# Strassen's algorithm for most of the first batch's up projections, and partial sums kept in a PSUM bank

## The chip, the cores and the metric

The kernel runs on one core of a Trainium2 chip. The metric is the device time of one execution in microseconds, from a few runs of the same kernel. The core has a matrix engine (PE in the profile, its weight loads shown as PEld), a vector engine (DVE), a scalar engine (ACT), a general engine (POOL), and SP, which here issues the transfers. Each works through a queue of its own; they wait for one another through semaphores. PE writes to PSUM[...]; DVE and ACT read it from there.

## What is computed

A clustered attention, then a bilinear feed-forward network on its output. The reference, cut to what matters:

```python
# q, k, v: (4, 8, 768, 64); centroids: (8, 16, 64)
q_assign = argmax(einsum('bhsd,hcd->bhsc', q_n, c_n))
k_assign = argmax(einsum('bhsd,hcd->bhsc', k_n, c_n))
mask = q_assign[:, :, :, None] == k_assign[:, :, None, :]
scores = where(mask, scale * q @ k.T, -1e9)
x = softmax(scores) @ v            # to (3072, 512)
# w_a, w_b: (512, 1536); w_out: (1536, 512)
out = ((x @ w_a) * (x @ w_b)) @ w_out
```

The weights come as 64-bit floats and are rounded to 32-bit floats in the kernel.

## The kernel before

**Attention.** There are 4 batches and 4 pairs of heads in each, 16 pairs `p`. The 768 queries of a pair are two halves `hf` of 384, the keys six tiles `j` of 128. One unit is one half against one key tile for both heads of the pair; a group `g` is two units, so a pair has 6 groups and there are 96. For each group the main loop has PE compute the scores (`score`, L548: one-hot cluster vectors, then q and k), ACT the exponentials (L557), PE the product with v for the group before (`weigh`, L589), and DVE, from the fifth pair on with POOL, the sums over keys (`add_up`, L578). When a half is complete, PE sums over partitions (`denominators`, L612), ACT copies (L617), DVE transposes, inverts and transposes back (`normalize`, L632 to L639), and POOL multiplies the output with it (L644). At the start of the next group ACT reads the inverse once more (`check_inverses`, L652). The preparation of the next pair (transposes, similarities L365, cluster choice, one-hot vectors L479 to L485) is spread over the six groups of a pair.

**Weights.** The 36 weight tiles of 128 x 512 are loaded one after another into two `raw` tiles and rounded by `round_w`: four DVE steps (L280, L283, L287, L290), of which the first two read the high halves of the raw words and the last the low halves; ACT takes the absolute value of the high halves into a tile of its own (`size`, L294); POOL adds the rest (L295); and in the next group `flush_w` has DVE multiply the weight with whether its size is at least `SMALLEST` (L302), which sets subnormal weights to 0. A table `due` says in which group each tile is rounded.

**Feed-forward.** It is cut into pieces, kept in the queue `ffn`, and each group takes pieces until a budget of columns (`PER_GROUP`) is used up. Pieces of one batch run beside the attention of the next. For batches 1 to 3 the up projections use Strassen's algorithm in Winograd's form (`ffn_ups`): the features are taken in pairs of 128-column tiles, and each of 6 indices and 2 weights makes 7 products of four blocks instead of 8. DVE forms the combinations of x (`combine_x`, L739 and L751) and of the weights (L766). PE writes each product to one of three PSUM banks of the pool `ps_m` in turn. ACT copies the first product out (L807), and DVE adds every other one where it belongs (L793). For the second weight, POOL multiplies the two factors of the network (L798). Batch 0's up projections are plain (`ffn_block`): every piece is one feature tile for one half of the rows, with four chunks of the inner dimension in one bank; ACT copies the first factor (L690) and DVE multiplies (L694). The first half's first pieces start when its own rows are ready, three groups before the second half's. All down projections (`ffn_downs`) use Strassen's algorithm.

**Order and buffers.** The order of each engine's instructions is that of the program. Scores have two tiles of two banks (`ps_s`), the outputs one bank (`ps_o`), and the remaining three banks (`ps_m`) serve similarities, denominators and all feed-forward products in turn. All feed-forward matmuls go through `in_halves` (L663), which splits the 128 output rows into two halves; the profile has two records for each matmul call in full precision.

Of the kernel before, what the change touches and what calls it, by code (L numbers as in the profile page):

```python
# [28 lines left out]
SMALLEST = 1.125 * 2.0 ** -15  # L29

# [5 lines left out]
def kernel(  # L36
# [97 lines left out]
    with tc.If(redo > 0):  # L134
        with ExitStack() as slow:
            long_path(nc, tc, slow, c, q, k, v, out)


def short_path(nc, tc, ctx, c, cn, centroids_in, casts, n_far, q, k, v,
# [32 lines left out]
    sizep = pool("sizep", 2)  # L172
# [96 lines left out]
    flush = []  # L269

    def round_w(i):
        flush_w()
# [20 lines left out]
        size = sizep.tile([P, WN], FP32, name="size")  # L293
        nc.scalar.activation(out=size, in_=halves(FP32)[:, :, 1], func=AF.Abs)  # L294
        nc.gpsimd.tensor_tensor(out=w, in0=w, in1=rest, op=ALU.add)  # L295
        flush.append((w, size))

    def flush_w():

        while flush:  # L300
            w, size = flush.pop(0)
            nc.vector.scalar_tensor_tensor(out=w, in0=size, scalar=SMALLEST,  # L302
                                           in1=w, op0=ALU.is_ge, op1=ALU.mult)

    stat = zero.tile([P, 4 * NPAIR], FP32, name="stat")
# [23 lines left out]
    def keep_busy(n):  # L329

        for _ in range(n):
            nc.tensor.transpose(out=idle[:, 0:P], in_=ident, identity=ident)  # L332

# [25 lines left out]
    def prep_sim(p):  # L359
# [3 lines left out]
        ps = ps_m.tile([P, 512], FP32, name="m")  # L363
# [238 lines left out]
    def denominators(p, hf):  # L602


        ps = ps_m.tile([P, 512], FP32, name="m")
# [52 lines left out]
    def in_halves(ps, lhsT, rhs, start, stop):  # L658


        for a in range(2):
            half = slice(a * D, (a + 1) * D)
            nc.tensor.matmul(out=ps[half], lhsT=lhsT[:, half], rhs=rhs,  # L663
                             start=start, stop=stop)
# [7 lines left out]
    def ffn_block(b, blk):  # L672

        box = {}
        t0 = blk * HB

        def up(w_sb, f):
            ps = ps_m.tile([P, 512], FP32, name="m")
            for ch in range(NCH):
                in_halves(ps[:, 0:HB], w_sb[:, ch, f * P:(f + 1) * P],  # L680
                          xTs[b][:, ch, t0:t0 + HB],
                          start=(ch == 0), stop=(ch == NCH - 1))
            return ps

        def piece_a(f):
            if f == 0:
                box["h"] = hp_.tile([P, NF, HB], FP32, name="h")
            ps = up(wa_sb, f)
# [3 lines left out]
        def piece_b(f):  # L692
            ps = up(wb_sb, f)
            nc.vector.tensor_tensor(out=box["h"][:, f, :], in0=box["a"],  # L694
                                    in1=ps[:, 0:HB], op=ALU.mult)

        ups = [(NCH * HB, lambda f=f, piece=piece: piece(f))
               for f in range(NF) for piece in (piece_a, piece_b)]
        return ups, box
# [10 lines left out]
    def room():  # L710
        if not W:
            W["raw"] = [rawp.tile([P, 2 * WN], FP32, name="raw") for _ in range(2)]
            W["size"] = [sizep.tile([P, WN], FP32, name="size") for _ in range(2)]
            W["comb"] = combp.tile([P, 2 * P], FP32, name="comb")
        return W["raw"], W["size"], W["comb"]
# [4 lines left out]
    def up_room():  # L720
        raw, size, comb = room()
        quarter = lambda t: t[:, 0:2 * HB].rearrange("p (c t) -> p c t", c=2)
        beside = lambda t: t[:, 2 * HB:].rearrange("p (c f) -> p c f", c=2)
        chunks = lambda t: [t[:, c, :] for c in range(2)]
        W["T3"], W["T2"] = chunks(quarter(raw[0])), chunks(quarter(raw[1]))
        W["T4"] = [t[:, 0:HB] for t in size]
        W["slots"] = [chunks(beside(raw[0])), chunks(beside(raw[1])),
                      chunks(comb.rearrange("p (c f) -> p c f", c=2)),
                      [t[:, HB:] for t in size]]

    def combine_x(b):
        up_room()
        x = xTs[b]
        for c in range(2):
            x11, x12 = x[:, c, 0:HB], x[:, c, HB:S]
            x22 = x[:, c + 2, HB:S]
            t2, t3 = W["T2"][c], W["T3"][c]
            for out, l, r in ((t3, x22, x12), (x12, x12, x11), (t2, x22, x12)):
                nc.vector.tensor_tensor(out=out, in0=l, in1=r, op=ALU.subtract)  # L739

    def ffn_ups(b, h):

        x = xTs[b]
        X = {"11": [x[:, c, 0:HB] for c in (0, 1)],
             "T1": [x[:, c, HB:S] for c in (0, 1)],
             "21": [x[:, c, 0:HB] for c in (2, 3)],
             "22": [x[:, c, HB:S] for c in (2, 3)]}

        def combine_t4():
            for c in range(2):  # L750
                nc.vector.tensor_tensor(out=W["T4"][c], in0=W["T2"][c],  # L751
                                        in1=X["21"][c], op=ALU.subtract)

        def products(w_sb, i, is_a):
            N2 = NF // 2
# [5 lines left out]
            def combine(name, l, r, op):  # L761

                at = {"S1": 1, "S2": 2, "S3": 0, "S4": 3}[name]
# [9 lines left out]
            def half_2():  # L773
# [3 lines left out]
                W["slots"] = [s[1], s[2], s[0], s[3]]  # L777

            def product(l, r):
                ps = ps_m.tile([P, 512], FP32, name="m")  # L780
                rhs = X[r] if r in X else W[r]
                for c in range(2):
                    in_halves(ps[:, 0:HB], A[l][c], rhs[c],
                              start=(c == 0), stop=(c == 1))
                return ps[:, 0:HB]
# [6 lines left out]
            def add(out, in0, ps, op=ALU.add):  # L792
                nc.vector.tensor_tensor(out=out, in0=in0, in1=ps, op=op)  # L793
# [7 lines left out]
            def p1():  # L801
# [3 lines left out]
                ps = product("11", "11")  # L805
                box["11"] = place(0, i)
                nc.scalar.copy(out=box["11"], in_=ps)  # L807

            def p6():
                ps = product("S2", "T2")  # L810
                box["12"] = place(1, i)
                add(box["12"], box["11"], ps)

            def p2_ahead():
                box["P2"] = product("12", "21")

            def p2():
# [552 lines left out]
```

## Time and profile before

| | |
|---|---|
| median of 3 runs (lowest, highest) | 1049.01 us (1048.68, 1049.04) |
| the profiled execution | 1048.94 us, of which its span is 1047.2 us |
| granted TensorE clock | 0.999 of full speed |

In a table of windows a line has the window, its length, and for each engine the busy time and, in brackets, the number of instructions; then the clock, the share of time in which the transfer engines work, and what they moved.

```profile
78.00:104.00 26.00, 26.00 (x171) 11.15 (x168) 22.82 (x42) 15.34 (x28) 4.86 (x4) 1.00 0.46 95
...
208.00:234.00 26.00, 26.00 (x164) 11.48 (x162) 21.69 (x34) 10.28 (x19) 13.76 (x13) 1.00 0.24 77
...
468.00:494.00 26.00, 26.00 (x168) 11.17 (x168) 17.14 (x33) 6.26 (x12) 11.30 (x12) 1.00 0.31 47
```

The order of engines is PE, PEld, DVE, ACT, POOL. The first window lies in the attention of batch 0 without any feed-forward work, the second in the first batch's up projections, while weights are still being rounded, the third in the second batch's Strassen products. PE's ends are modelled, so 26 of 26 us says that matmuls follow one another closely, not that they are at their peak.

In the page's groups of instructions, a line has the source line, the engine, the operation, what it writes and reads, its shape and count; then busy time and mean duration in ns; then the idle time of the engine just before, and who ended it. In a timeline, it is the start, the time, the engine, the line, the operation, and in square brackets the idle time before and who ended it.

### The profile page before, as it was taken

The numbers are of one execution on the slowest core, as the hardware profiler recorded it, in microseconds if no ns is written. First come the engines' busy times: TensorE is split into PE (matmuls) and PEld (weight loads), VectorE is DVE, ScalarE is ACT, GpSimd is POOL, SyncE is SP. The second block draws the span as 40 slices with busy tenths as digits, with TensorE's granted clock in tenths as the row PEclk, the third lists the DMA queues.
The fourth block names the chain that finished last, engine by engine and source line by source line (L and its number), as shares of the span: only waits on it lengthen the run. The fifth ranks groups of instructions, "written<-read, shape, count | busy, mean of one in ns | idle before, by whom it ended". The sixth has DMA issues, their size and how long they took to land.

```text
span 1047.2 us, 17953 instructions
## 1 busy us (share of the span) xinstructions
PE 1034.4 (99%) x7163; PEld 510.5 (49%) x7163; DVE 710.3 (68%) x1404; ACT 259.8 (25%) x500; POOL 355.8 (34%) x329
## 2 busy tenths in 40 slices
PE   9999999999999999999999999999999999999997
PEld 5444444444445554444444555444444565444575
DVE  6778877887857457676766736767655846776752
ACT  4665333233321221221212121222121200000000
POOL 1111345555543332453545422453344310212200
PEclk9999999999999999999999999999999999999999
DMA  7334243525130221203020030200000000000001
GB/s 182 87 84 88 85 107 105 126 71 140 63 49 21 43 38 29 32 5 46 5 46 6 25 62 25 46 1 20 1 4 2 15 28 22 1 1 1 2 32 34
DMA packets 120523, 46.49 MB, mean 44 GB/s; under 512 B 106608, under 2 KB 115824, under 8 KB 120432
## 3 DMA queue, kind: packets, MB, share of 16 engines
q1 hardware_dynamic: 120016, 44.85, 18.4%
q8 instruction: 58, 0.95, 0.4%
q10 hardware_dynamic: 416, 0.43, 0.1%
q14 instruction: 33, 0.27, 0.1%
HBM read 37.78 MB, written 6.29 MB: 42 GB/s over the span
## 4 chain that ended last, share of the span: by engine, by line
PE 93%; DVE 4%; issue 1%; POOL 1%; ACT 0%; DVEq 0%; POOLq 0%
PE m L663 61%; PE s L548 15%; PE O L589 12%; PE m L612 2%; PE m L365 1%; DVE raw L739 1%; POOL xT L644 1%; DVE raw L766 0%; PE m L346 0%; DVE xT L739 0%; PE O L332 0%; DVE ha L793 0%; DVE acc L639 0%; DVE raw L883 0%; DVE acc L578 0%
## 5 line engine op out<-in xcount | busy, mean ns | idle before, releaser
L557 ACT ACTIVATE pt<-s 128x768 f32<-128x768 f32 x192 | 145.2, 808 | 307.0 <-PE s L548 245.3
L578 POOL TENSOR_TENSOR acc<-acc,pt 128x384 f32<-128x384 f32 x144 | 152.8, 1075 | 57.8 <-ACT pt L557 41.8
L798 POOL TENSOR_TENSOR h<-h,ha 128x384 f32<-128x384 f32 x72 | 73.0, 1022 | 230.9 <-DVE ha L793 226.4
L589 PE MATMUL O<-pt,v 128*64 128x384 f32 x768 | 145.0, 499 | 0.0
L548 PE MATMUL s<-qkT 64*128 64x384 f32 x768 | 139.7, 482 | 0.0
L663 PE MATMUL m<-xT,wa_sb 128*64 128x384 f32 x672 | 119.3, 487 | 1.7 <-POOL xT L644 0.9
L663 PE MATMUL m<-xT,wb_sb 128*64 128x384 f32 x672 | 119.2, 487 | 0.0
L793 DVE TENSOR_TENSOR ha<-ha,m 128x384 f32<-128x384 f32 x126 | 66.8, 546 | 70.6 <-PE m L663 69.6
L793 DVE TENSOR_TENSOR h<-h,m 128x384 f32<-128x384 f32 x126 | 67.2, 549 | 61.1 <-PE m L663 60.3
L578 DVE TENSOR_TENSOR acc<-acc,pt 128x384 f32<-128x384 f32 x96 | 73.6, 793 | 36.1 <-POOL acc L578 35.1
L589 PEld LDWEIGHTS O<-pt,v 128*64 128x64 f32 x768 | 46.7, 136 | 85.8 <-issue 85.6
L663 PE MATMUL m<-wo_sb,h 128*64 128x256 f32 x768 | 86.8, 379 | 0.0
L548 PEld LDWEIGHTS s<-qkT 64*128 64x128 f32 x768 | 70.5, 187 | 31.3 <-issue 0.2
L644 POOL TENSOR_TENSOR xT<-xT,acc 128x384 f32<-128x384 f32 x32 | 33.0, 1032 | 142.6 <-DVE acc L639 142.6
L663 PEld LDWEIGHTS m<-xT,wa_sb 128*64 128x64 f32 x672 | 49.3, 137 | 61.3 <-issue 50.5
L663 PEld LDWEIGHTS m<-xT,wb_sb 128*64 128x64 f32 x672 | 48.9, 137 | 60.1 <-issue 54.3
L663 PE MATMUL m<-raw 128*64 128x384 f32 x384 | 70.3, 487 | 1.1 <-DVE ha L793 1.1
L663 PEld LDWEIGHTS m<-wo_sb,h 128*64 128x64 f32 x768 | 57.0, 137 | 29.0 <-issue 3.8
L663 PE MATMUL m<-xT,h 128*64 128x256 f32 x576 | 64.8, 379 | 0.1
L663 PEld LDWEIGHTS m<-xT,h 128*64 128x64 f32 x576 | 43.0, 137 | 21.0 <-issue 2.9
L663 PE MATMUL m<-xT,size 128*64 128x384 f32 x288 | 52.6, 486 | 0.0
L548 PE MATMUL s<-ohT 64*128 64x384 bf16 x384 | 48.2, 328 | 0.0
(166 smaller groups left out, 1267.1 us busy)
## 6 DMA issues: line engine op xcount, KB each, us to landing
raw<-in_moe_w_a_dram SPq DMA_DIRECT2D x12, 512.0 KB, 4.0
raw<-in_moe_w_b_dram SPq DMA_DIRECT2D x12, 512.0 KB, 3.6
raw<-in_moe_w_out_dram SPq DMA_DIRECT2D x12, 512.0 KB, 3.7
qk<-in_q_dram SPq DMA_DIRECT2D x48, 96.0 KB, 3.2
qk<-in_k_dram SPq DMA_DIRECT2D x48, 96.0 KB, 3.6
v<-in_v_dram SPq DMA_DIRECT2D x24, 192.0 KB, 3.8
out_dram<-rest SPq DMA_DIRECT2D x24, 128.0 KB, 1.7
v<-in_v_dram SPq DMA_DIRECT2D x4, 384.0 KB, 4.6
```

Of the source, the lines that this page charges most:

```text
L365: nc.tensor.matmul(out=ps[32 * kq:32 * kq + 32, 0:HB], lhsT=cTb[:, hp, :], rhs=qkTs[p][:, kq * HB:(kq + 1) * HB], start=True, stop=True)
L548: nc.tensor.matmul(out=s[:, a, 0:HB], lhsT=Ts[p][r, S + j * P:S + (j + 1) * P], rhs=Ts[p][r, hf * HB:(hf + 1) * HB], start=start, stop=not ...
L557: nc.scalar.activation(out=pt, in_=s[:, :, 0:HB], func=AF.Exp, scale=SCALE)
L578: eng.tensor_tensor(out=acc[:, a, :], in0=probs[u - 1][:, a, :] if j == 1 else acc[:, a, :], in1=probs[u][:, a, :], op=ALU.add)
L589: nc.tensor.matmul(out=O_of[0][a * D:(a + 1) * D, 0:HB], lhsT=vs[p][:, a, j, :], rhs=probs[u][:, a, :], start=(j == 0), stop=(j == NJ - 1))
L612: nc.tensor.matmul(out=ps[a * D:(a + 1) * D, 0:HB], lhsT=ones, rhs=t[:, a, :], start=(n == 0), stop=(n == len(terms) - 1))
L644: nc.gpsimd.tensor_tensor(out=x, in0=x, in1=den, op=ALU.mult)
L663: nc.tensor.matmul(out=ps[half], lhsT=lhsT[:, half], rhs=rhs, start=start, stop=stop)
L739: nc.vector.tensor_tensor(out=out, in0=l, in1=r, op=ALU.subtract)
L793: nc.vector.tensor_tensor(out=out, in0=in0, in1=ps, op=op)
L798: nc.gpsimd.tensor_tensor(out=to, in0=to, in1=box[name], op=ALU.mult)
```

## The change

1. Batch 0: feature tiles 0 to 7 of 12 (indices 0, 1, 4, 5, each with the tile two further on) go through `ffn_ups` too. The last four stay plain (`plain_ups`), both halves one after the other. Nothing of batch 0 starts before the second half of pair 3 is ready. The combinations of x for batch 0 stand in those rows of the result tiles `h` that the plain pieces write last; those and the first weight combinations are spread over groups 14 to 24 (`early_steps`), and the rest follows when the half is ready.
2. In all Strassen products the three banks are held for good (`in_turn`) and named X, Y, Z. P1, P6, P7 and P4 add up in X, and ACT copies X out after each (`take`); P2 and P3 go to Y, P5 to Z, and DVE adds those. T4 has the other sign, so P4 can be added. For the second weight DVE multiplies the last sum with the first factor straight from X. The order is P1, P2, P6, P5, P7, P3, P4. Weight combinations for the next part come after P7 and P4.
3. Denominators and similarities take a score tile (`apart`) once the three banks are held.
4. `round_w` no longer has the DVE step L302 and its tile. ACT takes the absolute value in place, in the raw tile, and then Relu of a steep straight line with a sum over the row in `stat`: it exceeds `LIMIT` where a weight is too small, and then the general path (`long_path`), which runs only when `stat` says so, loads the weights again and sets the small ones to 0.
5. The due times of the later weights and the budget per group of batch 0 are changed to match.

```diff
-        size = sizep.tile([P, WN], FP32, name="size")
-        nc.scalar.activation(out=size, in_=halves(FP32)[:, :, 1], func=AF.Abs)
+        size = halves(FP32)[:, :, 1]
+        nc.scalar.activation(out=size, in_=size, func=AF.Abs)
         nc.gpsimd.tensor_tensor(out=w, in0=w, in1=rest, op=ALU.add)
-        flush.append((w, size))
-
-    def flush_w():
-
-        while flush:
-            w, size = flush.pop(0)
-            nc.vector.scalar_tensor_tensor(out=w, in0=size, scalar=SMALLEST,
-                                           in1=w, op0=ALU.is_ge, op1=ALU.mult)
+        n = 4 * NPAIR + i
+        nc.scalar.activation(out=size, in_=size, func=AF.Relu, scale=-STEEP,
+                             bias=edge[:, 0:1], accum_out=stat[:, n:n + 1])
...
+    banks = []
+
+    def apart():
+        if banks:
+            return ps_s.tile([P, 2, 512], FP32, name="s")[:, 0, :]
+        return ps_m.tile([P, 512], FP32, name="m")
...
+    def in_turn():
+
+        if not banks:
+            banks.extend(ps_m.tile([P, 512], FP32, name="m") for _ in range(3))
+        banks.append(banks.pop(0))
+        return banks[-1]
...
+    def early_room(h):
+        pair, other, comb = spare()
+        W["slots"] = [two(pair[:, 0:2 * P]), two(pair[:, 2 * P:]), two(comb),
+                      two(other[:, 0:2 * P])]
+        h.extend(hp_.tile([P, NF, HB], FP32, name="h") for _ in range(2))
+        for n, name in enumerate(("T1", "T2", "T3", "T4")):
+            k, f = divmod(2 * n, 4)
+            W[name] = [h[k][:, NF - 4 + f + c, :] for c in range(2)]
+
+    def combination_x(b, name, c):
+        x = xTs[b]
+        l, r = {"T3": (x[:, c + 2, HB:S], x[:, c, HB:S]),
+                "T1": (x[:, c, HB:S], x[:, c, 0:HB]),
+                "T2": (x[:, c + 2, HB:S], W["T1"][c]),
+                "T4": (x[:, c + 2, 0:HB], W["T2"][c])}[name]
+        nc.vector.tensor_tensor(out=W[name][c], in0=l, in1=r, op=ALU.subtract)
...
+        N2, firsts = (NF // 2, range(NF // 2)) if b else (2, (0, 1, 4, 5))
...
-            def product(l, r):
-                ps = ps_m.tile([P, 512], FP32, name="m")
+            def product(name, l, r, start=True):
+                ps = box[name]
                 rhs = X[r] if r in X else W[r]
                 for c in range(2):
                     in_halves(ps[:, 0:HB], A[l][c], rhs[c],
-                              start=(c == 0), stop=(c == 1))
-                return ps[:, 0:HB]
+                              start=(start and c == 0), stop=(c == 1),
+                              skip_group_check=not start)
...
+            def take(name, k, f):
+                box[name] = place(k, f)
+                nc.scalar.copy(out=box[name], in_=box["X"][:, 0:HB])
+
+            def add(name, bank):
+                nc.vector.tensor_tensor(out=box[name], in0=box[name],
+                                        in1=box[bank][:, 0:HB], op=ALU.add)
...
-                ps = product("11", "11")
-                box["11"] = place(0, i)
-                nc.scalar.copy(out=box["11"], in_=ps)
+                for name in ("X", "Y", "Z"):
+                    box[name] = in_turn()
+                banks.reverse()
+                product("X", "11", "11")
+                take("11", 0, i)
+
+            def p2():
+                product("Y", "12", "21")
+                add("11", "Y")
+                done("11", 0, i)

             def p6():
-                ps = product("S2", "T2")
-                box["12"] = place(1, i)
-                add(box["12"], box["11"], ps)
+                product("X", "S2", "T2", start=False)
+                take("12", 1, i)
+
+            def p5():
+                product("Z", "S1", "T1")
+                add("12", "Z")
...
             def p7():
+                product("X", "S3", "T3", start=False)
+                take("22", 1, i + N2)
+                add("22", "Z")
+                done("22", 1, i + N2)
+
+            def p3():
+                product("Y", "S4", "22")
+                add("12", "Y")
+                done("12", 1, i)

             def p4():
+                product("X", "22", "T4", start=False)
+                if is_a:
+                    take("21", 0, i + N2)
+                    return
+                to = h[0][:, i + N2, :]
+                nc.vector.tensor_tensor(out=to, in0=to, in1=box["X"][:, 0:HB],
+                                        op=ALU.mult)
...
+            return half_1, half_2, [p1, p2, p6, p5, p7, p3, p4]
...
             if n + 1 < len(parts):
                 ps[4] = both(ps[4], parts[n + 1][0])
+                ps[6] = both(ps[6], parts[n + 1][1])
...
+        return {HP * GPP - 10: both(begin, T("T1", 0)), HP * GPP - 8: T("T1", 1),
+                HP * GPP - 4: T("T3", 0), HP * GPP - 3: T("T2", 0),
+                HP * GPP - 2: T("T4", 0), HP * GPP - 1: lambda: by_name[0](),
+                HP * GPP: lambda: by_name[1]()}
...
+            h = h_first
+            for name in ("T3", "T2", "T4"):
+                combination_x(0, name, 1)
+            ffn.extend(ups_first + plain_ups(0, h, range(NF - 4, NF)))
...
     PER_GROUP = [int(cols / n) + 1 for cols, n in (
-        (UP + DOWN * 7 / 8, BG + 5.8), ((UP + DOWN) * 7 / 8, BG + 0.8),
+        (UP * 11 / 12 + DOWN * 7 / 8, BG + 2.8), ((UP + DOWN) * 7 / 8, BG + 0.8),
...
-        due.setdefault(23 + int((i - 8) / 1.5), []).append(i)
+        due.setdefault(25 + int((i - 8) / 1.45), []).append(i)
```

(HP is 4, GPP 6, NF 12, HB 384, S 768.)

## The prediction

> **What bounds the kernel now.** I read the page's busy shares first, then the windows, then the timelines of single engines, because a busy PE alone doesn't say that PE works at its own pace.
>
> ```profile
> PE 1034.4 (99%) x7163; PEld 510.5 (49%) x7163; DVE 710.3 (68%) x1404; ACT 259.8 (25%) x500; POOL 355.8 (34%) x329
> ...
> L663 PE MATMUL m<-xT,wa_sb 128*64 128x384 f32 x672 | 119.3, 487 | 1.7 <-POOL xT L644 0.9
> ```
>
> PE is the bound. DVE is busy two thirds of the time, ACT one quarter. The timeline of PE shows the pace of the up projections and the rare holes:
>
> ```profile
> 109.33 1.51 PE L589 MATMUL O<-pt,v 128*64 128x384 f32 x8
> 110.67 2.10 PE L663 MATMUL m<-xT,wa_sb 128*64 128x384 f32 x12
> 113.66 0.87 PE L663 MATMUL m<-xT,wa_sb 128*64 128x384 f32 x4 [0.89 <-POOL xT L644]
> 114.36 2.75 PE L663 MATMUL m<-xT,wb_sb 128*64 128x384 f32 x16
> ...
> 122.68 0.81 PE L612 MATMUL m<-pt,ones 128*64 128x384 f32 x4
> 123.98 1.01 PE L612 MATMUL m<-acc,ones 128*64 128x384 f32 x3 [0.48 <-DVE acc L578]
> ...
> 165.16 2.75 PE L663 MATMUL m<-xT,wb_sb 128*64 128x384 f32 x16
> 167.85 0.50 PE L548 MATMUL s<-ohT 64*128 64x384 bf16 x4
> 168.18 1.45 PE L548 MATMUL s<-qkT 64*128 64x384 f32 x8
> 169.56 1.51 PE L589 MATMUL O<-pt,v 128*64 128x384 f32 x8
> 170.91 2.75 PE L663 MATMUL m<-xT,wa_sb 128*64 128x384 f32 x16
> ```
>
> From start to start, a plain piece of 16 records takes 2.58 us (170.91 to 173.49), so a record takes 0.161 us and a Strassen product of 8 records 1.29 us. A group spends 3.06 us on scores and weighing (167.85 to 170.91), plus 0.64 us for denominators in some groups. I counted start-to-start intervals over the ordinary 0.33 us in the whole span: the lost time is about 6 us. The large ones are 1.0 us at 113.66 and 0.65 us at 123.98 (first FFN pieces), 0.6 us at 397.03 and 646.55, and 0.7 us at 508.77 and 758.29 (batches 1 and 2).
>
> So the time is PE's sum plus whatever PE has to wait for. What can make it wait is DVE, which is late just where the first batch's FFN begins:
>
> ```profile
> 107.77 0.54 DVE L481 TENSOR_TENSOR oh<-sim,first 64x384 bf16<-64x384 f32 x1
> 110.39 0.58 DVE L485 STREAM_TRANSPOSE oh<-oh 128x384 bf16<-128x384 bf16 x1 [2.08 <-POOL oh L479]
> ...
> 112.23 2.73 DVE L578 TENSOR_TENSOR acc<-acc,pt 128x384 f32<-128x384 f32 x4
> ...
> 119.81 0.42 DVE L280 TENSOR_SCALAR wb_sb<-raw 128x512 int32<-128x512 int32 x1
> 120.27 0.69 DVE L283 SCALAR_TENSOR_TENSOR wb_sb<-raw,wb_sb 128x512 int32<-128x512 int32 x1
> ```
>
> The last two steps belong to the weight tile whose Abs ACT had already done at 115.60: ACT was 5 us ahead of DVE, which costs nothing as long as that Abs waits for its DMA alone.
>
> [...]ACT stood 1.97 us before L652 at 112.34 for DVE's L639, with an Abs whose data was there behind it. [...]L578 on DVE takes 0.55 us alone and 1.34 us beside POOL at 170.81. [...]
>
> **The change, part by part.**
>
> *Fewer matmuls.* Of batch 0's 12 feature columns, 8 go by Strassen: 4 indices x 2 weights = 8 parts, each 7 products of 8 records instead of 8 x 8. That is 8 x 8 = 64 records x 0.161 = 10.3 us off PE. The program's order of instructions has these counts, so this part does what it says.
>
> *Later start.* The first pieces come at group 26 instead of 23. PE's sum is unchanged. The two holes at 113.66 and 123.98 go with their places (-1.65), and what is late instead is worked out below.
>
> *L302 goes* (36 x about 0.97 us on DVE, 35 us in all), with its waits for POOL. Off the path by itself. In its place ACT does Abs in the raw tile and then a Relu with a sum: 36 x (0.69, as Abs, + 0.2, as L617's read of the accumulator) = 32 us. Nothing if ACT only runs. **But Abs now overwrites what DVE's L280 and L283 read, so it must wait for L283**, and behind it in ACT's queue stand the next exps and, new, the copies that free PSUM banks.
>
> *A kept bank.* P1, P6, P7, P4 add up in one bank X, and ACT copies it out after each. Only one other product lies between, so the copy must end within 1.29 us of the product's end. From the trace (batch 3): last matmul of P1 starts 896.82, ACT's copy runs 897.35 to 897.83; the next use would start at 898.43. Slack 0.6 us when ACT is free. Before, three banks went round and a reader could be 2.58 us late. In batches 1 to 3 ACT's exps end before the first FFN piece of a group (170.60 against 170.91), no weights are rounded, and DVE loses per pair of parts 5 adds; there I count no new stall, and count the holes at 508.77 and 758.29, where DVE was late, as gone (-1.4). Bounds: gain 2.5 if those at 397.03 and 646.55 go too, loss up to 11 if each of the 36 parts' 3 uses is 0.1 us late.
>
> *Edits at nothing.* Denominators and similarities take a score tile (`apart`): they come after the exps have emptied it, and the next scores come 6 us later, behind FFN pieces; without these they would wait about 1 us for ACT's copy. A raw tile is free about 1 us later for the next weight's DMA: landing takes 4 us, and with two tiles and groups of 10 us PE never sees it; at the worst it adds to the rounding's delay. The weights' due times move by 2 groups with the start. The loop in `long_path` isn't reached by this data: the trace of before has no line of it.
>
> *DVE in batch 0.* Per Strassen pair of parts DVE gets 16 combinations (0.41 us each, the union of L766 over 288) and 9 adds (0.47 when queued) = 10.8 us per 14 products. At 4.85 products a group (a budget of 3725 columns, 768 for each) that is 3.7; rounding 1.45 tiles a group at 2.33 us (L280 to L290) 3.4; sums, transposes, one-hots and normalising 2.25, from the same rows. Together 9.4 us against PE's 9.7 us a group: no reserve, where before it was 7.8 to 9.5.
>
> **The start, walked through.** In groups 22 to 25 DVE's work is at first as in the trace, since a combination of x replaces an L302. DVE finishes the POOL-bound L485 at 111.0, one combination and normalising by 112.9, four sums by 115.5, half of the weight combinations by 116.4, and the last two sums of pair 3 by 117.4. PE, with no FFN to fill groups 23 to 25, wants those sums for its denominators at 114.6: stall 2.8 us. Then DVE has two transposes and the other half (2.8), a sum, two tiles to round (0.8 + 4.8), L473 and normalising (2.0), POOL's multiplication (1.2), three combinations (1.9), a sum (0.8), and L280 and L283 of the next tile (1.15): 132.8. Only then may ACT do Abs, Relu and the copy of P1 (0.7 + 0.9 + 0.5, with handovers 2.15): P6 can start at 135. PE, having done P1 and P2, is there at 127.7: stall 7.2 us. Sum 10.0; bounds 3 (DVE a tenth quicker, and the early Abs not last) and 12.
>
> **The groups after it.** A group with two tiles to round has this order on ACT: exps, Abs/Relu, a copy, Abs/Relu, a copy. DVE starts the group's sum up to 3 us after the group (170.81 for 167.85, waiting for POOL), then rounds (L283 at +5.5), does combinations and the second tile (L283 at +9). The second Abs, Relu and copy end at +11; PE wants the bank at about +7 to +9. I walked groups 27 to 33 in this way: 1.8, 0, 2.9, 0, 2.3, 0, 3.7, then 2.3 for the last three with Strassen: 13.0. Each stall lets DVE catch up, and I have charged POOL's contention everywhere, so I take four fifths, 10.4. Bounds 3 and 16. The plain pieces after them have 2.58 us a piece and two banks of slack, and lose nothing.
>
> **Sum.** The profiled execution took 1048.94 us, of which 1.74 lie around the span; the median of the runs is 1049.01, 0.07 more, which I leave aside. 1048.94 - 10.3 - 1.65 - 1.4 + 10.0 + 10.4 = 1056.0.
>
> **Rivals.**
> - *The forecast: ACT waits for DVE, and PE for ACT, in the first batch.* For it: ACT was 3 to 5 us ahead of L283, and DVE has no reserve. 1051 to 1064, chance 0.52.
> - *Faster: DVE stays abreast.* The place is L283 in groups 25 to 36. Without L302 DVE no longer waits 1 to 1.4 us for POOL after each tile (119.20), so L283 could be done before ACT gets to Abs. Then the start costs 3 and the groups 2.5: 1048.94 - 13.35 + 5.5 = 1041.1. It decides where both stalls together stay under 11 us. Against it: the sums above. Chance 0.28.
> - *Even.* The stalls are about as large as the savings of 13.35, 11 to 15.5 us: 1047 to 1051. Chance 0.12.
> - *The kept bank costs in all batches*, the 36 x 3 copies being 0.1 us late: 11 more, 1067. Against it: the 0.6 us of slack. Chance 0.08.
>
> **How the numbers follow.** A measurement tells 0.2% (2.1 us) from no change. Slower 0.52 + 0.08 = 0.60, same 0.12, faster 0.28. The likeliest case's own range is 1051 to 1064; with the other sign holding more than a quarter, the range must reach down to the faster case, 1041 to 1064, and leaves out its lower part and the last rival.
>
> **What would show it.** PE's records on ups 64 fewer. Idle time of PE before the products of the first batch, released by ACT's copies, of about 7 us once and 2 to 4 us several times; 2 to 3 us before L612's counterpart in pair 3; ACT idle before Abs, released by DVE. From about 270 us on the two traces should run alike up to the shift. I am wrong if ACT's Abs isn't kept waiting by DVE, or if PE's idle time before 260 us stays under 11 us.

## The result, and the profile after

| | before | after |
|---|---|---|
| median (lowest, highest) | 1049.03 us (1048.68, 1049.46) | 1077.58 us (1077.52, 1077.86) |
| ratio, 95% interval | | 1.0272 [1.0255, 1.029] |
| span of the profiled execution | 1047.2 us | 1076.2 us |
| granted TensorE clock | 0.999 | 0.988 |
| matmul records | 7163 | 7099 |

The change costs 28.6 us; the forecast was 7 us. The page of after, busy shares and the slices of the span (each digit is the busy share of a fortieth of the span in tenths, here some 27 us; PEclk is the granted clock in the same form):

```profile
PE 1034.9 (96%) x7099; PEld 500.0 (46%) x7099; DVE 681.7 (63%) x1371; ACT 338.9 (31%) x674; POOL 343.5 (32%) x323
...
PE   9999778978999999999999999999999999999997
...
DVE  6778887868677756656455855755554755454652
...
PEclk9999889989999999999999999999999999999999
```

PE has 64 records fewer, as it should, but is busy as long as before (1034.9 us after 1034.4), and the span is 29 us longer. The digits say where: in slices 5 to 10, from about 108 to 269 us, PE is idle for up to 30% of the time, and in three of these slices its clock is not at full speed. Everything after 290 us looks as before. The timeline of PE shows the waits themselves (start, time, engine, line, operation, and in square brackets the idle time before and who ended it):

```profile
111.95 1.51 PE L595 MATMUL O<-pt,v 128*64 128x384 f32 x8
117.20 0.33 PE L554 MATMUL s<-ohT 64*128 64x384 bf16 x1 [3.75 <-DMA ohT<-oh]
119.73 0.82 PE L554 MATMUL s<-ohT 64*128 64x384 bf16 x3 [2.19 <-DMA ohT<-oh]
120.02 3.08 PE L554 MATMUL s<-qkT 64*128 64x384 f32 x8
...
141.38 2.76 PE L676 MATMUL m<-h,pair 128*64 128x384 f32 x8 [5.19 <-ACT h L824]
...
230.96 2.83 PE L676 MATMUL m<-h,comb 128*64 128x384 f32 x8 [4.76 <-ACT ha L824]
233.58 2.77 PE L676 MATMUL m<-h,pair 128*64 128x384 f32 x8
```

Two things are to be seen. Two waits are for the one-hot vectors of pair 4, the first pair of batch 1, and the others are for a copy of ACT (L824), which empties bank X. And behind a long wait a Strassen product of 8 records takes 2.76 to 2.83 us, where it takes 1.46 at full speed: PE works at half its pace for a while. The table of windows shows the same (window, length, busy time and number of PE, PEld, DVE, ACT and POOL, then the clock, the share of the transfers and what they moved):

```profile
122.00:126.00 4.00, 4.00 (x18) 1.27 (x16) 2.68 (x7) 1.97 (x3) 1.38 (x1) 0.70 0.69 113
126.00:141.00 15.00, 10.20 (x68) 3.98 (x64) 13.36 (x20) 8.12 (x18) 7.45 (x7) 1.00 0.51 120
141.00:146.00 5.00, 4.62 (x18) 1.89 (x20) 2.29 (x5) 0.81 (x2) 4.51 (x4) 0.66 0.34 105
...
231.00:237.00 6.00, 6.00 (x22) 2.23 (x24) 1.75 (x5) 0.48 (x1) 3.52 (x4) 0.50 0.31 87
```

Why the copy was late at 141.38 stands in ACT's timeline:

```profile
139.41 0.67 ACT L294 ACTIVATE raw<-raw 128x512 f32<-128x512 f32 x1 [5.68 <-DVE wa_sb L282]
140.11 0.77 ACT L297 ACTIVATE raw<-raw,edge 128x512 f32<-128x512 f32 x1
140.77 0.20 ACT L297 ACTIVATION_READ_ACCUMULATOR raw<-raw,edge 128x1 f32 x1
140.86 0.47 ACT L824 COPY h<-m 128x384 f32<-128x384 f32 x1
```

ACT stood idle for 5.68 us, with a copy behind it that PE was waiting for, because the first instruction in its queue was the Abs in place (L294), and this may not overwrite the raw words before DVE's L282 has read them. In the list of waits (in total, times, longest):

```profile
ACT raw L294 <- DVE wa_sb L282: 15.7, 5, 5.7
...
ACT raw L294 <- DVE wo_sb L282: 12.7, 8, 2.0
...
PE m L676 <- ACT h L824: 10.5, 4, 5.2
...
PE m L676 <- ACT ha L824: 9.6, 4, 4.8
...
ACT raw L294 <- DVE wb_sb L282: 9.0, 4, 3.3
...
PE m L676 <- DVE ha L827: 3.5, 4, 2.2
```

**The account.** I took what PE's start-to-start intervals have beyond the ordinary 0.33 us, and put those with idle time before them under waits, the others under half pace. Intervals of up to 0.42 us without idle time, where one kind of product follows another, are left out; they come to nearly the same in both kernels (16.7 and 16.6 us).

| | before | after |
|---|---|---|
| waits, first 104 us (exponentials late at 37, 63 and 90 us, in after alone) | 1.05 | 4.09 |
| waits, 104 to 160 us | 1.68 | 13.78 |
| waits, 160 to 290 us | 0 | 16.52 |
| waits, from 290 us on | 3.55 | 2.49 |
| half pace | 0 | 8.43 |

The waits come to 30.6 us more, half pace to 8.4, and the 64 records, by the forecast's 0.161 us each, to 10.3 less: 28.7 together, against 28.6 in the medians and 29.0 between the two spans.

### The profile page after: what moved, and what is told of

It reads as the page before. It is cut to its first block, busy times and chain, and to the rows that moved or that the text cites. A ratio compares the mean times of both kernels' runs of the same rounds, so it can differ in the third digit from the quotient of the medians.

```text
span 1076.2 us, 17860 instructions
## 1 busy us (share of the span) xinstructions
PE 1034.9 (96%) x7099; PEld 500.0 (46%) x7099; DVE 681.7 (63%) x1371; ACT 338.9 (31%) x674; POOL 343.5 (32%) x323
## 4 chain that ended last, share of the span: by engine, by line
PE 82%; DVE 11%; ACT 3%; issue 2%; POOL 1%; DMA 1%; SPq 0%; DVEq 0%; POOLq 0%
PE m L676 56%; PE s L554 12%; PE O L595 10%; PE s L618 1%; DVE acc L584 1%; DVE pair L794 1%; ACT raw L297 1%; DVE comb L794 1%; ACT raw L294 1%; PE s L371 1%; DVE raw L762 1%; ACT pt L563 1%; PE m L618 1%; DVE other L794 1%; DVE ha L827 0%
## 5 line engine op out<-in xcount | busy, mean ns | idle before, releaser
L833 POOL TENSOR_TENSOR h<-h,ha 128x384 f32<-128x384 f32 x66 | 67.8, 1029 | 275.6 <-DVE ha L827 275.6
L827 DVE TENSOR_TENSOR ha<-ha,m 128x384 f32<-128x384 f32 x88 | 48.3, 549 | 113.7 <-PE m L676 82.0
L824 ACT COPY h<-m 128x384 f32<-128x384 f32 x88 | 41.9, 477 | 204.2 <-PE m L676 202.1
L827 DVE TENSOR_TENSOR h<-h,m 128x384 f32<-128x384 f32 x88 | 48.2, 548 | 89.6 <-PE m L676 56.3
L676 PE MATMUL m<-xT,wa_sb 128*64 128x384 f32 x480 | 84.3, 488 | 4.4 <-DVE ha L827 3.5
L676 PE MATMUL m<-xT,wb_sb 128*64 128x384 f32 x480 | 83.0, 486 | 0.0
L676 PE MATMUL m<-raw 128*64 128x384 f32 x432 | 78.9, 487 | 0.0
L824 ACT COPY ha<-m 128x384 f32<-128x384 f32 x66 | 31.5, 477 | 99.0 <-PE m L676 98.2
L676 PEld LDWEIGHTS m<-xT,wa_sb 128*64 128x64 f32 x480 | 33.7, 137 | 49.3 <-issue 37.3
L676 PEld LDWEIGHTS m<-xT,wb_sb 128*64 128x64 f32 x480 | 34.5, 137 | 42.9 <-issue 38.8
```

The source lines that it names most:

```text
L824: nc.scalar.copy(out=box[name], in_=box["X"][:, 0:HB])
L827: nc.vector.tensor_tensor(out=box[name], in0=box[name], in1=box[bank][:, 0:HB], op=ALU.add)
L833: nc.gpsimd.tensor_tensor(out=to, in0=to, in1=box[name], op=ALU.mult)
```

## The experiments

Theory A is that of the forecast: ACT's queue is held by an Abs that waits for DVE. The questions beside it: what else is late, why PE ran at half pace, and what the kept bank alone is worth.

**1. The Abs in a tile of its own.** In the first batch the upper half of a tile of weight combinations is free; Abs and Relu write there, so that Abs waits only for its transfer.

```diff
-        size = halves(FP32)[:, :, 1]
-        nc.scalar.activation(out=size, in_=size, func=AF.Abs)
+        size = spare()[1][:, WN // 2:].bitcast(BF16)
+        nc.scalar.activation(out=size, in_=halves(FP32)[:, :, 1], func=AF.Abs)
```

> The changed kernel, but ACT's Abs and Relu go to a piece of a tile of ACT's own (the upper half of a combination tile, as bf16), so that Abs waits for its DMA alone and not for DVE's L282. Theory A (ACT's queue, held by DVE through the write in place, keeps PE from its bank): the waits of PE for ACT's copies in the first batch (5.2, 2.2, 3.6, 1.2, 4.8, 0.5, 1.9, 0.8 us at 141 to 269) mostly go, and the slow stretches behind them too: 1052 to 1060 us. Theory B (DVE has no reserve, whoever waits for whom): the waits stay and only change their name to DVE: 1068 to 1077 us.

Measured: 1059.34 us, ratio 1.0101 [1.0084, 1.0118]. 18.2 us of the loss are gone with two lines. ACT's timeline at the same place:

```profile
133.81 0.69 ACT L294 ACTIVATE other<-raw 128x512 bf16<-128x512 f32 x1 [0.29 <-DMA raw<-in_moe_w_a_dram]
134.53 0.72 ACT L297 ACTIVATE other<-other,edge 128x512 bf16<-128x512 bf16 x1
...
135.25 0.46 ACT L824 COPY h<-m 128x384 f32<-128x384 f32 x1
```

The copy of P1 runs 5.6 us earlier. By the account above, waits are 13.9 us and half pace is 5.2 us less than in after. The list of waits:

```profile
PE m L676 <- DVE ha L827: 7.3, 5, 3.9
...
PE m L676 <- DVE h L827: 2.5, 1, 2.5
...
PE m L676 <- ACT ha L824: 0.3, 1, 0.3
```

PE's waits for ACT have fallen from 20.1 us to 0.3, and those for DVE's adds (L827, which free banks Y and Z) have grown from 3.5 to 9.8. So the in-place Abs was the first cause, and DVE is next behind it. Windows of the same run, the third bracket being DVE:

```profile
142.00:162.00 20.00, 17.55 (x100) 7.31 (x100) 19.51 (x33) 9.87 (x20) 11.10 (x10) 0.91 0.28 80
...
182.00:202.00 20.00, 16.05 (x94) 6.36 (x92) 19.62 (x32) 6.31 (x13) 10.15 (x10) 0.91 0.63 138
```

DVE works 98% of the time in these two windows, and 93% from 122 to 262 us, where the kernel before has 83% in its window from 208 to 234 us.

**2. The Abs in place, but last in its group.** Abs, Relu and the next load move behind the group's copies.

```diff
-        nc.scalar.activation(out=size, in_=size, func=AF.Abs)
...
+        def measure():
+            nc.scalar.activation(out=size, in_=size, func=AF.Abs)
...
+            load_w(i + 2)
+        deferred.append(measure)
```

> The changed kernel with Abs and Relu still in place but issued at the end of each group, behind the copies of that group, and the load of the next weight tile behind them. Theory A: by then DVE's L282 is done, ACT isn't held: 1052 to 1062 us. Theory B: 1068 to 1077 us. The price of its own: raw tiles come free up to 9 us later, so the rounding can be late (DVE waiting for raw's DMA).

Measured: 1061.01 us, ratio 1.0118 [1.0101, 1.0135]. The same gain to 1.7 us, with the same operands and the same wait, and only another place in ACT's queue. What cost the time was what stood behind the Abs, not the Abs.

**3. The rounding alone.** The kernel before with the changed rounding and the longer general path; the feed-forward is untouched.

```diff
-        size = sizep.tile([P, WN], FP32, name="size")
-        nc.scalar.activation(out=size, in_=halves(FP32)[:, :, 1], func=AF.Abs)
+        size = halves(FP32)[:, :, 1]
+        nc.scalar.activation(out=size, in_=size, func=AF.Abs)
...
-    def flush_w():
...
+        nc.scalar.activation(out=size, in_=size, func=AF.Relu, scale=-STEEP,
+                             bias=edge[:, 0:1], accum_out=stat[:, n:n + 1])
```

> The kernel before with the changed rounding alone (Abs in place, Relu with a sum on ACT, no L302; the general path as in the changed kernel), with plain up projections in the first batch and the old banks. Theory A: no bank waits for ACT's copy with a single product between, so little is lost: 1048 to 1052 us, with about 3 us of waits for ACT's exps in the first 104 us, less what DVE's relief saves. Rival (the in-place rounding costs by itself, through late exps): 1060 us or more.

Measured: 1050.60 us, ratio 1.002 [1.0014, 1.0027], 2.0 us above the kernel before. So the rounding alone costs 2.0 us, the other edits without the write in place cost 10.8 (experiment 1), and all of them together 28.6: some 16 us come from the pair. What the rounding costs alone begins in the attention of batch 0. ACT, and then PE, of this run:

```profile
33.67 0.67 ACT L294 ACTIVATE raw<-raw 128x512 f32<-128x512 f32 x1
34.37 0.78 ACT L297 ACTIVATE raw<-raw,edge 128x512 f32<-128x512 f32 x1
35.04 0.19 ACT L297 ACTIVATION_READ_ACCUMULATOR raw<-raw,edge 128x1 f32 x1
35.13 0.78 ACT L431 COPY ohT<-m 128x768 bf16<-128x768 bf16 x1
35.81 1.51 ACT L555 ACTIVATE pt<-s 128x768 f32<-128x768 f32 x2
```

```profile
36.67 0.34 PE L546 MATMUL s<-ohT 64*128 64x384 bf16 x2 [0.35 <-ACT pt L555]
37.37 0.34 PE L546 MATMUL s<-ohT 64*128 64x384 bf16 x2 [0.36 <-ACT pt L555]
```

Relu and its accumulator read add 0.97 us ahead of the exponentials, in a group in which a copy of one-hot vectors (L431) comes as well; the next scores wait for the tile that the exponentials empty. This happens in three of the eight groups with a weight tile, at 37, 63 and 90 us: 0.9 us each, and in after they make 2.6 of the 3.0 us by which the account's first line grows (the other 0.4 is a wait for a sum at 81 us). One more wait, of ACT and then of PE, is the one that the forecast described, with plain pieces:

```profile
147.75 0.69 ACT L294 ACTIVATE raw<-raw 128x512 f32<-128x512 f32 x1 [4.79 <-DVE wb_sb L283]
...
149.22 0.84 ACT L688 COPY ha<-m 128x384 f32<-128x384 f32 x2
```

```profile
149.73 2.48 PE L661 MATMUL m<-xT,wb_sb 128*64 128x384 f32 x14 [1.28 <-ACT ha L688]
```

It is the only one of its kind. By the account the waits of this run are 3.7 us longer than before, while the time is 2.0 us longer; where the rest comes back I did not follow.

**4. PE kept running in its waits.** Before four of the waits of after PE gets 16 to 24 transposes of the identity, whose results nobody uses. Theory C is that the half pace comes from the wait before it. In after it stands behind waits of 2.19 to 5.19 us, with the clock at 0.50 to 0.72 in the windows after them, but not behind one of 2.17 us at 207.93, where the clock stays at 1.00.

```diff
+    def filler(n):
+        ps = apart()
+        for _ in range(n):
+            nc.tensor.transpose(out=ps[:, 0:P], in_=ident, identity=ident)
+
+    FILL = {(0, 2): 24, (2, 4): 16, (5, 2): 21}
...
+        if g == BG:
+            filler(17)
```

> The changed kernel with idle transposes of 128x128 put where PE waits longest, into a bank that nobody reads: 17 before the scores of group 24, 24 before P6 of the first part, 16 before P7 of the third, 21 before P6 of the sixth. They should fit into the waits. Theory C [...]: the stretches at half pace behind these four waits go, some 6.5 us: 1069 to 1073 us. Rival (the pace after a wait has another cause, say the operands' arrival): 1077 us or more, and the stretches stay.

Measured: 1074.67 us, 2.9 below after, between theory C's 1069 to 1073 and the rival's 1077. The fillers shortened the four waits but did not fill them. Two of them in this run:

```profile
140.95 2.83 PE L683 MATMUL m<-h,pair 128*64 128x384 f32 x8 [2.64 <-ACT h L831]
...
181.14 1.51 PE L683 MATMUL m<-h,pair 128*64 128x384 f32 x8 [1.76 <-ACT h L831]
```

At 181 us 1.76 us were left of 3.62, and the product behind the wait runs at full pace: the clock is 1.00 from 181 to 187 us, where after has 0.66 from 182 to 187. At 141 us 2.64 were left of 5.19 and at 231 us 2.31 of 4.76, and at 117 us a second wait of 2.20 followed the shortened one; behind these three the half pace stayed, as it did behind the wait of 2.18 at 157 us, which had no filler (clock 0.72 from 157 to 163 us). Over the span half pace fell from 8.4 to 5.6 us, which is the whole gain. So the half pace went where the wait was brought under 2 us. That was one wait of the four, and this experiment alone proves no more than that.

**5. Other groups for the first eight weights**, with the Abs in its own tile from here on.

```diff
-    due = {3 * i + 1: [i] for i in range(8)}
+    due = {max(3 * i - 1, 1): [i] for i in range(8)}
```

> The changed kernel with the Abs in a tile of its own, as in e1_own_tile, and with the first eight weights rounded in groups 1, 2, 5, 8, 11, 14, 17, 20 instead of 1, 4, 7, ... 22. Theory D (two collisions in the order of the groups): the 5.8 us that PE waits at group 24 for the one-hot vectors of pair 4 come from the weight tile of group 22, which stands on DVE and POOL ahead of them (2.3 us and 2 us), and the 3 us at 37, 64 and 91 us from groups in which ACT has a copy of one-hot vectors as well as Abs and Relu before the exponentials. Then the waits at group 24 shrink to 2 us or less, those three go, and the time is 1051 to 1055 us. Rival (DVE is late anyway, whatever stands in group 22, and the exponentials are late by Relu in any group): 1057 us or more.

Measured: 1055.59 us, ratio 1.0065 [1.0049, 1.0082], 3.8 below experiment 1. The waits for exponentials at 37, 63 and 90 us are gone, as expected. The wait for the one-hot vectors shrank from 5.8 us to 2.4, but another appeared, in PE's timeline:

```profile
107.34 1.33 PE L618 MATMUL m<-acc,ones 128*64 128x384 f32 x4 [2.76 <-DVE acc L584]
...
117.70 0.49 PE L554 MATMUL s<-ohT 64*128 64x384 bf16 x3 [2.20 <-DMA ohT<-oh]
```

The tile that left group 22 stands in group 20 now, and there the sums of pair 3 are late. Another of 0.8 us, also for a sum, came at 29 us. Half of theory D, then: the place was right, but the tile is in the way in group 20 too, and the time is just above the 1051 to 1055 us expected.

**6. Slower rounding, and half the combinations on POOL.** First the weights 8 to 23 at 1.3 instead of 1.45 a group, the rest faster later; then also the combinations S3 and S4 of the first batch on POOL.

```diff
-        due.setdefault(25 + int((i - 8) / 1.45), []).append(i)
+        g = 25 + int((i - 8) / 1.3) if i < 24 else 37 + int((i - 24) / 1.75)
+        due.setdefault(g, []).append(i)
```

> As e5_other_groups, with the weights 8 to 23 spread at 1.3 a group instead of 1.45 from group 25 on, and the last twelve at 1.75 a group from group 37, when the Strassen products of the first batch are over. Theory E (what PE still waits for in groups 27 to 37 is DVE, which has more to do than fits in a group): 0.15 tiles x 2.3 us less a group over 12 groups is 4 us less on DVE, and the time is 2 to 4 us below e5_other_groups. Rival (the remaining waits come from the order within a group, not from the sum): within 1 us of e5_other_groups.

> As e6_slower_rounding, with the weight combinations S3 and S4 of the first batch on POOL instead of DVE: 8 of 16 for each pair of parts, at 0.28 to 0.41 us each on DVE 1 to 1.6 us less a group there. Theory E: 1 to 3 us below e6_slower_rounding. Rival (DVE and POOL hinder each other, or the products wait for POOL, which is busy with sums): 0 to 5 us above it.

Measured: 1050.71 us, ratio 1.0023 [1.0015, 1.0032], for the first, 4.9 below experiment 5: theory E, and a little more than its 2 to 4 us. In the two profiles the waits are 5.1 us shorter in sum, and half pace is the same (2.8 and 3.0 us): a stretch behind the wait at 146 us is gone, and one behind the wait at 107 us is new. The second took 1054.51 us, ratio 1.0057 [1.004, 1.0074], 3.8 above the first, as its rival had it. I did not separate the two reasons that the rival names.

**7. The kept bank alone.** The kernel before with the new Strassen products in batches 1 to 3; first batch and rounding as before.

```diff
-                ps = product("S2", "T2")
-                box["12"] = place(1, i)
-                add(box["12"], box["11"], ps)
+                product("X", "S2", "T2", start=False)
+                take("12", 1, i)
```

> The kernel before with the kept bank alone: the new order of the Strassen products of batches 1 to 3, three banks held for good from the first batch's down projections on, denominators and similarities in a score tile from there; the first batch's up projections and the rounding are those of before. Theory F (from 290 us on the changed kernel gains: its shift against before falls from 30.97 us at 428 us to 28.99 at the end): 1046 to 1048 us. Rival (the last rival of the prediction, the kept bank costs in all batches): 1050 us or more.

Measured: 1046.88 us, ratio 0.9984 [0.9977, 0.9991]: 1.7 us below the kernel before, and faster than both kernels of this case, if only by 0.2% (highest of 20 runs 1047.74, lowest of 33 of the kernel before 1048.18). Before and here the products' large holes at 397, 508, 646 and 757 us are alike (0.9 to 1.0 us from start to start), so the gain is not where the forecast had put it. Of the 2.65 us between the two profiled spans, by the starts of the groups, about 0.5 arise before group 20, which the edit doesn't touch, 0.9 in small amounts between groups 45 and 95, and 1.2 behind the last group, where the hole of 0.7 us at 882.90 is gone.

**8. No weight in group 20 either, and the second tile of a group last.**

```diff
+    due = {g: [i] for i, g in enumerate((1, 3, 5, 7, 9, 11, 14, 17))}
...
-                round_next()
```

> As e6_slower_rounding, but the first eight weights are rounded in groups 1, 3, 5, 7, 9, 11, 14, 17, so that none falls in group 20 either. Theory D: the 2.8 us wait for the sums of pair 3 at 107 us in e6_slower_rounding comes from the tile rounded in group 20 together with two combinations of x, and goes, with up to 1.5 us of half pace behind it: 1047 to 1049 us. Rival (DVE is as late with any tile in the 20 groups before, since it is nearly full there): 1050 us or more.

> As e10_tile7, and in groups with two weight tiles the second is rounded after the group's last FFN piece instead of after its first. Theory G (the waits at 146 and 192 us come from the order within a group: the second tile's 2.3 us stand on DVE ahead of the adds that free banks Y and Z): 2 to 5 us below e10_tile7, 1043 to 1047 us. Theory E alone (only the sum of DVE's work counts): within 1 us of e10_tile7.

With the first line alone (on top of experiment 6): 1048.63 us, ratio 1.0011 [0.9999, 1.0022], level with the kernel before, as expected. With the second as well: 1055.73 us, ratio 1.0066 [1.0049, 1.0083], 7 us worse where theory G had hoped for 2 to 5 better. The largest wait that was left without the second edit, DVE and then PE:

```profile
186.82 0.38 DVE L279 TENSOR_SCALAR wb_sb<-raw 128x512 int32<-128x512 int32 x1
187.23 0.69 DVE L282 SCALAR_TENSOR_TENSOR wb_sb<-raw,wb_sb 128x512 int32<-128x512 int32 x1
188.03 0.43 DVE L286 TENSOR_SCALAR rest<-wb_sb 128x512 int32<-128x512 int32 x1
188.49 0.69 DVE L289 SCALAR_TENSOR_TENSOR rest<-raw,rest 128x512 f32<-128x512 uint32 x1
189.10 0.55 DVE L827 TENSOR_TENSOR ha<-ha,m 128x384 f32<-128x384 f32 x1
```

```profile
185.73 1.46 PE L676 MATMUL m<-xT,wa_sb 128*64 128x384 f32 x8
189.70 2.83 PE L676 MATMUL m<-xT,wa_sb 128*64 128x384 f32 x8 [2.51 <-DVE ha L827]
```

The four steps of a weight tile stand in front of the add that PE waits for, as theory G says. With the second edit this wait is 0.18 us. But in the other order the steps of the second tile stand in front of the next group's sum (at 159.82 and 164.57 us in that run), which also waited for POOL there, and PE's waits come back elsewhere (169 us: 2.44, 208 us: 1.74, 225 us: 1.86, each for an add). That they come from the late sums is likely, and not shown.

**9. The one-hot vectors a group earlier, and P1's copy before the Abs in group 26.**

```diff
-                    assign[:2], assign[2:], [one_hot, one_hot_across], []]
+                    assign, [one_hot, one_hot_across], [], []]
...
-        round_next()
+        if g != BG + 2:
+            round_next()
```

> As e10_tile7, with the one-hot vectors of pair 4 made one group earlier (all four assignment steps in group 20, the vectors and their transfers in group 21). Theory D: PE's wait of 2.2 us for the transfers of the vectors at 115.5 us goes, as the transfers have a group more: 1045.5 to 1047.5 us, and the runs lie closer together if it was this wait that sometimes brought the half pace. Rival (DVE has the same work by then, so the sums of pair 3 or its combinations are late instead): 1048 us or more.

> As e11_early_onehot, and in group 26, where the first batch's products begin, the weight tile is rounded after P1 instead of before it. Theory A in a third form: in e10_tile7 ACT stood 1.7 us before that tile's Abs because its transfer had not landed, with the copy of P1 behind it in the queue, and PE waited 1.5 us for the copy. With the copy ahead of the Abs this wait goes: 1 to 2 us below e11_early_onehot. Rival (DVE's combinations of x, which PE's P6 needs as well, end no earlier): within 0.5 us of it.

Measured: 1048.47 us, ratio 0.9997 [0.9989, 1.0006], with the first edit: nothing gained. The wait for the transfers went, and in its place PE waited 1.54 us for the sums of pair 3 at 107.73 and 0.7 us longer for P1's copy. The runs do lie closer together: 1047.7 to 1049.9 for all twelve, while four of the twelve of experiment 8's first kernel took 1052.0 to 1052.5. With the second edit 1050.19 us, ratio 1.0014 [1.0007, 1.0021]: PE waited 1.48 us for a combination of x (L762) instead of the copy, and later for an add. The first went as its rival had it. In the second the rival had the cause, DVE's combinations, but with 1.7 us above the first edit neither it (within 0.5 us) nor the theory had the size. In these experiments each wait that was taken away by order was followed by another for DVE.

## Why the forecast was wrong

The direction and the mechanism were right: ACT's Abs waited for DVE's L282, 37.4 us in 17 waits, and PE for ACT's copies, 20.1 us. The size was not. By the terms of its sum, in us:

| term | forecast | after |
|---|---|---|
| 64 fewer records | -10.3 | -10.3 |
| old holes at 113.66 and 123.98 | -1.65 | -1.65 |
| holes of batches 1 to 3 | -1.4 | -1.1 |
| the start | +10.0 | +11.4 |
| the groups after it | +10.4 | +18.9 |
| before 104 us, mostly exponentials late | 0 | +3.0 |
| half pace behind waits | 0 | +8.4 |
| sum | +7.1 | +28.7 |

**Fewer matmuls** came as counted.

**The holes of batches 1 to 3.** Those at 508.77 and 758.29, 0.7 us each, which I counted as gone, are still there with 0.66 us each; the one at 882.90 (0.6) and two smaller ones went instead. The sum is near by luck. That the kept bank costs nothing in batches 1 to 3 was right, and experiment 7 shows it by itself.

**The start** has about its size, but of other parts. The wait for P1's copy was 5.3 us where I had 7.2, by the mechanism I had walked through. But "PE, with no FFN to fill groups 23 to 25, wants those sums for its denominators at 114.6: stall 2.8 us" named the wrong customer. PE comes to the scores of pair 4 first. Their one-hot vectors went through DVE (L491) at 113.47 in after, and then through transfers; PE waited 6.1 us for them (117.20 and 119.73), and the sums were ready by then. I had followed DVE's list and not asked which of its products PE's own order needs first, and the transfers behind L491 were not in my walk. Before, feed-forward pieces of the first half stood in PE's queue at this place.

**The groups after it** are the term that failed most. I had walked them to 13.0 us and taken four fifths, because "Each stall lets DVE catch up". After has 18.9: seven waits for ACT's copies, 16.0 us, and two for DVE's adds, 2.8. So the walk was too short, and the discount made it worse. Its prices were too low. I had taken 0.41 us for a weight combination from the later batches, where the trace gives 0.38 (110.05 us for 288); in after the 64 of the first batch take 32.3 us, 0.50 each, an add 0.54 instead of 0.47, and a tile's four steps 2.40 instead of 2.33. With these my sum for DVE is, as an estimate, 10.2 us a group instead of 9.4, and no longer fits into PE's 9.7. If DVE is short in every group, what it makes up in one stall is used up in the next group. That this is why the discount failed is argued, not shown: experiment 1 has DVE at 98% in two such windows, but in after it is busy for only 116 of the 144 us from 126 to 270, where it waits in its turn for products of PE and copies of ACT. The plain pieces behind them lost nothing, as forecast.

**Half pace** was not in the forecast at all. I had put waits of 7.2 and 3.7 us into the sum without asking what PE does after them. In after the clock is 0.66 from 182 to 187 us, behind a wait of 3.62 us, and 0.50 from 231 to 237 us, behind one of 4.76. What the runs show of shorter waits stands in the last section.

**Exponentials late.** I priced Abs and Relu at 32 us of ACT and wrote "Nothing if ACT only runs". The groups before 104 us have no feed-forward pieces between the scores of one group and of the next, so an exponential that ends 1 us later is PE's wait in the three groups where ACT has another copy as well: 2.6 us in all.

**Edits at nothing.** That the later transfers of raw tiles are never seen by PE holds in after, where no Abs waits for one. It is not so in general: in experiment 8's first kernel ACT stands 1.69 us before an Abs at 129.22, released by the transfer of the raw tile, and PE waits 1.46 us for the copy behind it. Relu brought no further load of a table: after has two, 1.28 us each, at 1.74 and 4.29 us, and the kernel before has two, at 1.75 and 4.04. That denominators and similarities in a score tile cost nothing was right: no wait of PE over 0.3 us in after is at them once the banks are held.

**The rivals.** "Faster: DVE stays abreast" fell with ACT's waits for L282. "The kept bank costs in all batches" fell with experiment 7. Its value, 1067, was nearer to the result than the forecast, for another reason.

What stays open: whether experiment 8's second kernel lost its 7 us by late sums alone, how much of the loss with combinations on POOL is the two engines hindering each other (in the kernel before, L578 on DVE takes 0.55 us alone and 1.34 beside POOL at 170.81), and what else made the groups longer than my walk. A version with Strassen's products in the first batch that beats the kept bank alone was not found; the best of them is level with the kernel before.

## What to carry to other kernels

- An operation in place may have to wait for what still reads its tile: here the Abs for L282, 37.4 us in 17 waits. Before writing it so, look at what is queued behind it on its engine; half a tile elsewhere was worth 18 us here.
- When a busy engine gets more work and another engine's cover goes, ask for each of its results which one the bounding engine needs first, and don't discount a walk through stalls when the late engine has no reserve. Take its prices from the stage in question: a combination cost 0.50 us in the first batch and 0.38 in the others.
- Price a wait of PE above 2 us with the slow stretch that stood behind most such waits in these runs, 0.9 to 2.7 us, and look at the clock of the window after it, not only at the idle time.

## What the runs showed of the hardware

After short waits PE kept its pace in these runs, after long ones mostly not. In after, from 100 us on, no half pace followed any of nine waits between 0.34 and 1.87 us. Of three between 2 and 3 us, two were followed by it (2.19 us each, at 119.73 and 157.68 us; clock 0.70 from 122 to 126 and 0.72 from 157 to 163 us) and one was not (2.17 us at 207.93; clock 1.00 from 208 to 215 us). Of four over 3 us, three were followed by it (5.19, 3.62 and 4.76 us, at 141.38, 181.75 and 230.96; clock 0.66 from 141 to 146, 0.66 from 182 to 187 and 0.50 from 231 to 237 us); behind the fourth (3.75 us at 117.20) came a second wait, the one at 119.73.

Over after and the twelve experiments, from 100 us on, no half pace followed any of the 118 waits between 0.15 and 2 us (the longest was 1.87); it followed 18 of 30 between 2 and 3 us, and a single slow interval one more; of nine over 3 us six were followed by it, and the other three by a second wait within half a us, so that it could not show. The stretch begins at once or up to 2.5 us later, ends 2.8 to 6 us after the wait in most cases, and costs 0.9 to 2.7 us. What decides between 2 and 3 us is not shown.

The runs of one kernel (experiment 8, the first) go from 1047.7 to 1052.5 us, the four longest with a clock of 0.994 and the others with 0.995 to 1.000. The same stretches may be behind that, but it is not shown, as one run alone has a trace.
